# Twelve Strassen blocks in the first matrix, C11 begun by a copy between PSUM banks, and single score blocks in a re-ordered attention and MLP kernel

## The chip, the cores and the metric

The kernel runs on one NeuronCore of a Trainium2 chip. The metric is device time in microseconds, the median over runs; lower is better. A profiled execution gives a span, from the first to the last instruction, and the rows that this document quotes. Engines: PE is TensorE, DVE is VectorE, ACT is ScalarE, POOL is GpSimd, and SP is the SyncE queue that only issues DMAs.

## The reference

Windowed attention over 4 batches and 8 heads (768 positions, head size 64), then a two-matrix block with the gate h - tanh(h):

```python
scores = scale * np.matmul(q, k.transpose(0, 1, 3, 2))
keep = is_global | is_local        # 8 global keys, and the last 96 positions
scores = np.where(keep, scores + bias, -1e9)
a = softmax(scores)
attn = np.matmul(a, v)             # (4, 8, 768, 64) -> x: (3072, 512)
h = x @ w_in                       # 512 -> 2048
g = h - np.tanh(h)
out = g @ w_out                    # 2048 -> 512, float32
```

## The kernel before

**Turns.** The 3072 tokens are 24 tiles of 128, here called turns. Turns 0 to 3 are the first tiles of the four batches. A turn looks at its own keys and, unless it is the first of its batch, at those of the tile before, so it has one or two score blocks: 44 in all. Global keys are copied over the first 8 keys of the turns that no longer reach them (words K and V).

**Order.** Nothing is scheduled at run time. The string ORDER lists some thousand words, and every word issues one operation on its engine, in that order; HOMES gives each buffer and PSUM bank. Each engine runs its own instructions strictly in that order, so one that waits holds up all behind it on the same engine. A suffix names the engine where a word leaves a choice: `/a` ACT, `/d` DVE, `/p` POOL, `/s` SP.

**Attention words, for turn u.** `lq lk lv` load; the two first turns load float32 rows into a staging tile (keys from SP, queries from ACT; `load_rows`, L337) and `cq ck` cast them. `T`, `Te` transpose and copy out (turns 7 and up use a DMA transpose on SP). `B` adds the bias by matmul for the first four turns. `S` makes the scores: eight matmuls per block, with 64 rows in, in pairs on the two halves of the array (`a_S`, L391). `E` is the exponential on ACT, `M` the mask product on DVE, `AV` the product with v, `R` and `N` the normalisation, `X` and `Xe` the transposition of x (turns 8 and up by DMA on SP).

**First matrix.** Turns go in groups: 0 and 1 alone, 2 to 11 in pairs (groups 2 to 6), 12 to 23 in fours (groups 7, 8, 9). A plain unit is `m1` (matmuls, L477), `th` (tanh on ACT, L576), `g` (the gate on DVE, L590). For a group of four turns, a block of four feature tiles against 512 tokens may instead be a Strassen (Winograd) block: products `d1` to `d7`, each four matmuls of 256 columns (`in_product`, L522); copies `e0` to `e2` of a running sum in bank r (`d_copy`); adds `q11 q21 q22` (`d_add`, L544); sums of weights `v1` to `v4` for a block column and of tokens `y1` to `y4` for a group. DUNITS lists six such blocks: parts 1, 2, 3 of groups 8 and 9.

**Second matrix.** Always Strassen, over pairs of turns (2 x 2 blocks of 128 tokens, 1024 features, 256 outputs). `w1` to `w4` sum weights, `n1` to `n4` sum gates (`g_sum`, L619; n3 and n4 in place), `p1` to `p7` are products of eight matmuls each (`product`, L632), `a0 a1 a2` copy the running sum in bank r (`keep`, L650), `c11 c12 c21 c22` make the results (`result`, L653), `st` stores. Before, C11 is bank q (product 2) plus the copy a0 of product 1.

**Score runs.** From turn 8 on `S` takes three blocks at a time (THREES, L172 to L182); turns 4 to 7 take both of theirs at once. That makes 19 runs of score matmuls on PE.

Of the kernel before, what the change touches and what calls it, by code (L numbers as in the profile page):

```python
# [7 lines left out]
FP32 = mybir.dt.float32  # L8
# [9 lines left out]
lq.1 lk.1 zero rel ones.0 zero:7 dist lq.2 lq.0 lk.0 zero:7 zero:7 table lq.3 turn zero:7 first zero:7 lk.3 ident slopes  # L18
zero:7 zero:7 lk.2 ones.1 B.0 lv.1 cq.1/a ck.1/d bm.1 lv.0 T.1.1 em.1 lv.2 T.1.0 Te.1.1/d B.1 cq.0/a lv.3 Te.1.0/d
ck.0/a T.0.0 S.1 in.0 Te.0.0/a T.3.0 B.2 E.1.0 in.1 Te.3.0/d T.0.1 Te.0.1/d in.3 T.2.1 T.3.1 Te.2.1/a T.2.0 Te.3.1/d S.0  # L20
lq.4 Te.2.0/a AV.1 E.0.0 S.2 R.1 N.1/d in.2 B.3 E.2.0 lk.4 AV.0 S.3 R.0 N.0/d X.1 in.4 E.3.0 AV.2 Xe.1/d X.0 in.5 R.2
N.2/d bm.2 Xe.0/a AV.3 m1.1.0 lk.5 em.2 R.3 N.3/d X.2 m1.0.0 th.1.0 Xe.2/d X.3 lq.5 th.0.0 g.1.0 m1.0.2 Xe.3/a g.0.0
m1.1.2 th.0.2 m1.2.2 th.1.2 g.0.2 g.1.2 lv.4 m1.2.6 th.2.2 lk.6 g.2.2 T.4.0 th.2.6 m1.2.0 Te.4.0/a m1.1.4 lq.6 th.2.0
m1.0.4 lv.5 th.1.4 g.1.4 T.4.1 m1.2.4 Te.4.1/a g.2.0 th.0.4 S.4 th.2.4 g.0.4 out.1 m1.1.8 K.4/a E.4.0 g.2.6 m1.2.8
th.1.8 M.4.0 E.4.1 m1.0.8 g.1.8 th.2.8 out.0 M.4.1 m1.0.12 th.0.8 g.2.4 out.2 T.5.1 g.2.8 T.5.0 Te.5.1/a m1.1.12 out.3
Te.5.0/d th.0.12 g.0.8 S.5 lk.7 th.1.12 g.0.12 AV.4 E.5.0 g.1.12 lq.7 m1.2.12 n1.0/d E.5.1 lk.10 m1.2.10 M.5.0 lq.10
V.4/a R.4 m1.2.14 M.5.1 th.2.10 K.5/d N.4/d AV.5 th.2.14 T.6.1 X.4 R.5 Te.6.1/a T.6.0 N.5/d lq.9 Xe.4/a Te.6.0/d X.5 S.6
Xe.5/d g.2.14 m1.3.2 E.6.1 n3.0/d m1.3.10 g.2.10 lq.8 th.2.12 w1.1 th.3.2 p1.0 E.6.0 w1.0 m1.3.12 g.2.12 a0.0/a g.3.2
m1.3.4 lk.8 th.3.12 n2.0/d K.6/a th.3.10 m1.3.0 w2.0 m1.3.8 w4.0 w2.1 lk.9 p2.0 M.6.0 p6.0 lv.7 g.3.12 w3.1 T.7 m1.3.6
lv.6 a1.0/a c11.0 th.3.0 w3.0 p5.0 g.3.10 p7.0 a2.0/a n1.2/d th.3.4 g.3.0 p1.2 th.3.6 n2.2/d p2.2 a0.2/a w4.1 th.3.8  # L30
# [91 lines left out]
def kernel(  # L122
# [371 lines left out]
    def wsum(j, k):  # L494
        return four(("ws", j))[:, k - 1]
# [347 lines left out]
```

## Time and profile before

| What | Value |
|---|---|
| median of 3 runs | 203.38 us (201.31 to 203.54) |
| span of the profiled execution | 199.8 us |
| what the shown runs have beyond that span | 1.5 to 3.7 us |
| TensorE clock granted | 1.000 |
| busy PE, weight load, DVE, ACT, POOL | 193.1, 157.8, 178.6, 135.1, 75.3 us |
| DMA | 27.36 MB moved |

The profiled execution's own time is its span and what lies around it; the profile has no other figure for it.

How to read the rows. In the chain of waits a row is start, length, and what held the end of the program up at that time; `x16` counts instructions. In a table of waits: the waiting engine and line, what it waited for, the sum in us, how often, and the longest. In groups: line, engine, operation, output<-input, shapes and count, then busy time and the mean ns of one, then idle time before them. In windows each engine has its busy time and number of instructions. A DMA's landing is counted from its issue.

### The profile page before, as it was taken

The page shows a single profiled execution, that of the slowest core. Times are in us where ns is not written, and L with a number is a line of the kernel's source. Part 1 is how long each engine was busy: PE and PEld are TensorE (multiplying, and loading weights), DVE is VectorE, ACT ScalarE, POOL GpSimd, SP SyncE. Part 2 cuts the span into 40 slices and gives each one's busy share as a digit, 9 for nine tenths or more (in the row PEclk, how much of TensorE's full clock was granted, in tenths as well). Part 3 has the DMA queues.
Part 4 walks back from the last instruction along what each step waited for, and adds up shares of the span by engine and source line. Part 5 has one row for each costly group of instructions (what it writes and reads, how often), then busy time and mean ns, then how long its engine had stood idle before and what let it go on. Part 6 is the DMA issues. An engine that isn't in the chain of part 4 may idle for free.

```text
span 199.8 us, 5524 instructions
## 1 busy us (share of the span) xinstructions
PE 193.1 (97%) x2219; PEld 157.8 (79%) x2219; DVE 178.6 (89%) x348; ACT 135.1 (68%) x234; POOL 75.3 (38%) x97
## 2 busy tenths in 40 slices
PE   8799999999999999999999999999999999999992
PEld 2469998888888988988898655688898687888892
DVE  6487599999999999999999898999999999999942
ACT  3698898726569559758947789578778777464220
POOL 8987576350694057069207904702000100001110
PEclk9999999999999999999999999999999999999999
DMA  5999999999999999989996998994733101001233
GB/s 148 211 180 185 198 163 207 201 156 141 193 167 196 178 153 135 133 188 171 137 158 146 140 173 192 154 155 85 55 108 121 66 0 54 3 0 52 107 132 131
DMA packets 103545, 27.36 MB, mean 137 GB/s; under 512 B 93920, under 2 KB 101472, under 8 KB 103520
## 3 DMA queue, kind: packets, MB, share of 16 engines
q0 software_dynamic: 74048, 16.78, 89.5%
q1 hardware_dynamic: 28928, 9.70, 27.6%
q10 hardware_dynamic: 544, 0.52, 1.0%
q8 instruction: 17, 0.28, 0.5%
q14 instruction: 8, 0.07, 0.1%
HBM read 27.26 MB, written 6.29 MB: 168 GB/s over the span
## 4 chain that ended last, share of the span: by engine, by line
PE 85%; DVE 7%; DMA 3%; ACT 2%; issue 1%; ACTq 0%; DVEq 0%
PE ps L645 36%; PE ps L477 27%; PE ps L536 9%; PE ps L396 5%; PE ps L427 5%; DMA f<-in_q_dram 3%; DVE gall L590 2%; DVE x L444 2%; DVE mem L407 1%; PE ps L455 1%; ACT mem L403 1%; PE ps L320 1%; ACT mem L274 1%; PE ps L365 1%; ACT th L576 1%
## 5 line engine op out<-in xcount | busy, mean ns | idle before, releaser
L477 PE MATMUL ps<-xT,w_in_bf 128*128 128x256 bf16 (+2 forms) x544 | 69.0, 279 | 0.0
L477 PEld LDWEIGHTS <-w_in_bf 128*128 128x128 bf16 x544 | 47.2, 98 | 12.4
L576 ACT ACTIVATE th<-ps 128x512 f32<-128x512 f32 (+1 forms) x74 | 41.8, 591 | 18.7 <-PE ps L477 13.6
L590 DVE TENSOR_TENSOR gall<-ps,th 128x512 bf16<-128x512 f32 (+1 forms) x74 | 47.4, 668 | 6.0 <-ACT th L576 5.6
L645 PEld LDWEIGHTS <-gall 128*128 128x128 bf16 x488 | 46.4, 98 | 7.0
L662 POOL DMA_DIRECT2D out_dram<-ot x14 | 8.1, 580 | 102.5 <-ACT ot L274 52.4
L403 ACT ACTIVATE mem<-ps 128x1024 bf16<-128x1024 f32 x44 | 43.3, 1024 | 4.3 <-PE ps L396 4.2
L645 PE MATMUL ps<-w_out_bf,gall 128*128 128x256 bf16 (+1 forms) x296 | 36.3, 270 | 0.0
L274 ACT COPY sn<-ps 128x256 f32<-128x256 f32 x32 | 12.0, 375 | 20.3 <-PE ps L645 16.3
L645 PE MATMUL ps<-f,ss 128*128 128x256 bf16 x192 | 24.9, 273 | 0.0
L645 PE MATMUL ps<-wc,gall 128*128 128x256 bf16 x192 | 24.9, 273 | 0.0
L342 POOL DMA_DIRECT2D vb<-in_v_dram x24 | 21.5, 900 | 2.2 <-issue 1.0
L645 PEld LDWEIGHTS <-ss 128*128 128x128 bf16 x192 | 18.3, 98 | 2.8
L342 POOL DMA_DIRECT2D mem<-in_k_dram x20 | 17.9, 899 | 4.8 <-DMA w_out_bf<-in_moe_w_out_dram 3.1
L342 POOL DMA_DIRECT2D mem<-in_q_dram x20 | 18.1, 904 | 3.8 <-DMA w_out_bf<-in_moe_w_out_dram 3.0
L412 DVE TENSOR_TENSOR mem<-mem,mk 128x2048 bf16<-128x2048 bf16 x16 | 19.2, 1215 | 0.0
L659 DVE TENSOR_TENSOR ot<-ps,sn 128x256 f32<-128x256 f32 x36 | 14.7, 415 | 3.6 <-ACT sn L274 2.5
L444 DVE TENSOR_TENSOR x<-ps,rden 128x512 bf16<-128x512 f32 x23 | 15.8, 687 | 0.5
L274 ACT COPY mem<-ps 128x512 f32<-128x512 f32 (+1 forms) x22 | 12.7, 585 | 5.1 <-PE ps L536 3.9
L427 PEld LDWEIGHTS <-mem 128*128 128x128 bf16 x352 | 13.4, 97 | 2.1 <-ACT mem L403 0.5
L427 PE MATMUL ps<-vb,mem 128*128 128x65 bf16 x352 | 14.7, 193 | 0.0
L396 PE MATMUL ps<-mem 64*128 64x128 bf16 x352 | 13.1, 217 | 0.0
(78 smaller groups left out, 220.7 us busy)
## 6 DMA issues: line engine op xcount, KB each, us to landing
out_dram<-ot POOLq DMA_DIRECT2D x14, 256.0 KB, 2.8
vb<-in_v_dram POOLq DMA_DIRECT2D x24, 128.0 KB, 6.2
mem<-in_q_dram POOLq DMA_DIRECT2D x22, 128.0 KB, 6.3
mem<-in_k_dram POOLq DMA_DIRECT2D x22, 128.0 KB, 6.1
out_dram<-ot SPq DMA_DIRECT2D x9, 256.0 KB, 2.0
w_out_bf<-in_moe_w_out_dram POOLq DMA_DIRECT2D x4, 512.0 KB, 10.7
w_in_bf<-in_moe_w_in_dram POOLq DMA_DIRECT2D x4, 256.0 KB, 7.6
w_in_bf<-in_moe_w_in_dram POOLq DMA_DIRECT2D x2, 512.0 KB, 11.0
```

Source lines behind the costliest of these rows:

```text
L274: nc.scalar.copy(out=out, in_=in_)
L342: eng(e).dma_start(out=dst, in_=rows_of(src, u).rearrange("h p d -> p h d"))
L396: nc.tensor.matmul(bank(("s", u, o), hh)[:, p * P : (p + 1) * P], buf(("qk", back[u] if o else u))[r, 1, p, :], buf(("qk", u))[r, 0, p, :] ...
L403: nc.scalar.activation(d, banks(("s", u, o), 0, 1), AF.Exp, bias=0.0, scale=scale)
L412: nc.vector.tensor_tensor(out=t, in0=t, in1=mk[:, 1:3], op=ALU.mult)
L427: nc.tensor.matmul(t[:, h // (H // 2), h % (H // 2), :], buf(("p", u, o))[:, slot(h), :], buf(("v", back[u] if o else u))[:, h, 0 : Dh + 1 ...
L444: nc.vector.tensor_tensor(out=buf(("x", u)).rearrange("q (a h) d -> q a h d", a=2), in0=t[:, :, :, 0:Dh], in1=rden.to_broadcast([P, 2, H / ...
L477: nc.tensor.matmul(t[:, (f - f0) * n : (f - f0 + 1) * n], w_in_bf[j][:, c, fo : fo + P], x[:, c, 0:n], start=(c == 0), stop=(c == CD - 1),)
L536: nc.tensor.matmul(t[:, r * 2 * P : (r + 1) * 2 * P], w(r)[:, c], x[:, c], start=first and r + c == 0, stop=c == 1, skip_group_check=not f ...
L576: nc.scalar.activation(h_view(buf(("th", g, f0)), g, m), h_view(bank(("h", g, f0)), g, m), AF.Tanh, bias=0.0, scale=1.0)
L590: nc.vector.tensor_tensor(out=o, in0=v(h), in1=v(th), op=ALU.subtract)
L645: nc.tensor.matmul(bank((holder, a))[:, c0:c1], s(f), t(f)[:, c0:c1], start=first and f == 0, stop=f == HF - 1, skip_group_check=not first,)
```

## The change

The planner's ORDER and HOMES are new throughout, so nearly every engine's instructions stand in another order. The parts of the code:

- DUNITS has twelve blocks, all four parts of groups 7, 8 and 9. Plain `m1` units go from 74 to 50; each new block has seven products, three copies and two adds. Weight sums for part 0 and token sums for group 7 are added; the weight sums get a tile of their own, `ws`.
- C11 and q11 are no longer added by DVE. `a0` and `e0` copy bank r into bank q on ACT, and product 2 accumulates onto that (`first` is False). `q11` is gone; `c11` is a plain copy from bank q.
- The signs of the second matrix's sums are turned round so that n1 to n4 are all additions. Six `n3` and five `n4` become POOL DMAs that add onto their destination.
- A score block is a word of its own.
- `gall` keeps each turn's gates together, so a Strassen block's output is seen as two turns of 128 columns; `g_sum` then works on 1024 elements in a row.
- Fewer buffers: `mem` 20 for 23, `xT` 3 for 4, `ss` 3 for 5, masks 2 for 3. Stores go 4 to POOL and 22 to SP (before, 14 and 12).

```diff
-lq.1 lk.1 zero rel ones.0 zero:7 dist lq.2 lq.0 lk.0 zero:7 zero:7 table lq.3 turn zero:7 first zero:7 lk.3 ident slopes
+lq.1 lk.1 ones.1 rel lq.2 zero zero:7 zero:7 zero:7 zero:7 zero:7 zero:7 zero:7 turn slopes lk.0 lq.3 ones.0 dist lk.3
+first lk.2 ident cq.1/a bm.1 lv.1 lq.0 ck.1/d B.0 lv.0 em.1 T.1.1 lv.2 T.1.0 T.2.0 lv.3 Te.1.0/d Te.1.1/a B.1 Te.2.0/a
...
-    NM, NV, NG, NSS, NSN = 23, 12, 5, 5, 4
+    NM, NV, NG, NSS, NSN, NXT = 20, 12, 5, 3, 4, 3
...
-    DUNITS = [(8, 1), (8, 2), (8, 3), (9, 1), (9, 2), (9, 3)]
+    DUNITS = [(g, j) for g in range(7, 10) for j in range(4)]
...
-    gall = pool.tile([P, NG, CF, 2 * P], BF16, name="gall")
+    gall = pool.tile([P, NG, 2, CF, P], BF16, name="gall")
...
-    def a_S(xs):
-        for u, o in xs:
+    def a_S(u, o):
...
     def d_keep(g, j, k):
-        return buf(("k0", g, j)) if k == 0 else mems(("k12", g, j), FP32)[:, (k - 1) * 4 * P : k * 4 * P]
+        return d_bank(g, j, "q") if k == 0 else mems(("k12", g, j), FP32)[:, (k - 1) * 4 * P : k * 4 * P]
...
-            2: ("q", lambda r: w_in_of(a + r, 2), x_block(g, 2, 1), True),
+            2: ("q", lambda r: w_in_of(a + r, 2), x_block(g, 2, 1), False),
...
-        t = d_bank(g, j, part)
+        t = d_bank(g, j, part).rearrange("q (t r n) -> q t r n", t=2, r=2)
...
-                    t[:, r * 2 * P : (r + 1) * 2 * P], w(r)[:, c], x[:, c], start=first and r + c == 0, stop=c == 1,
+                    t[:, :, r, :], w(r)[:, c], x[:, c], start=first and r + c == 0, stop=c == 1,
...
     def d_add(g, j, k):
-        if k == 0:
-            q = d_bank(g, j, "q")
-            nc.vector.tensor_tensor(out=q, in0=q, in1=d_keep(g, j, 0), op=ALU.add)
-            return
...
-        eng(e).tensor_tensor(out=o(), in0=x(), in1=y(), op=op)
+        if e is POOL:
+            nc.gpsimd.dma_start(out=o, in_=y, accum_op=ALU.add)
+        else:
+            eng(e).tensor_tensor(out=o, in0=x, in1=y, op=ALU.add)
...
-            2: ("q", lambda f: g_of(a, HF + f), w(1, 0), True),
+            2: ("q", lambda f: g_of(a, HF + f), w(1, 0), False),
...
     def keep(e, a, k):
-        copy(e, buf(("sn", a, k)), bank(("r", a))[:, 0:DH2])
+        copy(e, buf(("sn", a, k)) if k else bank(("q", a))[:, 0:DH2], bank(("r", a))[:, 0:DH2])
...
-        if (i, j) == (1, 2):
-            copy(e, o, bank(("r", a))[:, c0:c1])
+        if i == 1:
+            copy(e, o, bank(("qr"[j - 1], a))[:, c0:c1])
             return
-        holder, k = {(1, 1): ("q", 0), (2, 1): ("z", 1), (2, 2): ("z", 2)}[i, j]
-        nc.vector.tensor_tensor(out=o, in0=bank((holder, a))[:, 0:DH2], in1=buf(("sn", a, k)), op=ALU.add)
+        nc.vector.tensor_tensor(out=o, in0=bank(("z", a))[:, 0:DH2], in1=buf(("sn", a, j)), op=ALU.subtract)
```

Three places in the instruction order. First, ACT at the start of the program, where the query rows of turns 1 and 0 are loaded into the staging tile (`f32`) and cast into `mem`; `mk` is a mask and `ps` PSUM. Before:

```order
L339 DMA f32_80<-in_q_dram 128x2x256 x2
L274 ACT_TABLE_LOAD
L274 CAST mem_81<-f32_80 128x512
L325 ACTIVATE mk_68<-ps_61 128x1024
L274 CAST mem_81<-f32_80 128x512 x2
L274 CAST mem_81<-ps_61 128x512
```

In the change:

```order
L332 DMA f32_80<-in_q_dram 128x2x256
L267 ACT_TABLE_LOAD
L267 CAST mem_81<-f32_80 128x512
L332 DMA f32_80<-in_q_dram 128x2x256
L318 ACTIVATE mk_68<-ps_61 128x1024
L267 CAST mem_81<-ps_61 128x512 x2
L267 CAST mem_81<-f32_80 128x512
```

The second query load, turn 0's, has moved behind the cast of the first, which waits for the first load to land.

Second, PE in the middle of the program: a score run (L396 before, L388 now) between matmuls of the second matrix (L645) and of Strassen blocks of the first (L529 now). Repeats are left out. Before, three blocks, 24 matmuls, in one run:

```order
L645 LDWEIGHTS ss_103
L645 MATMUL ps<-f_80,ss_103 128x256
L396 LDWEIGHTS mem
L396 MATMUL ps<-mem 128x128
...
L645 LDWEIGHTS ss_104
L645 MATMUL ps<-f_80,ss_104 128x256
```

In the change, one block, eight matmuls, between two products of a Strassen block:

```order
L529 LDWEIGHTS w_in_bf_74
L529 MATMUL ps<-xT_99,w_in_bf_74 128x2x128
L388 LDWEIGHTS mem
L388 MATMUL ps<-mem 128x128
...
L529 LDWEIGHTS ws
L529 MATMUL ps<-mem,ws 128x2x128
```

The runs have become shorter and there are 27 of them where there were 19; the output of a block matmul is now two runs of 128.

Third, POOL late in the program: loads of v (`vb`), stores (`ot`), and in the change the sums n3 and n4 (into `gall`). Before:

```order
L342 DMA mem_81<-in_k_dram 128x8x64
L342 DMA vb2_84<-in_v_dram 128x8x64
L342 DMA vb5_87<-in_v_dram 128x8x64
L662 DMA out_0_dram<-ot0_113 128x512
L342 DMA vb4_86<-in_v_dram 128x8x64
L342 DMA vb6_88<-in_v_dram 128x8x64
L662 DMA out_0_dram<-ot3_116 128x512
L342 DMA vb7_89<-in_v_dram 128x8x64
```

In the change:

```order
L624 DMA gall_102<-ss0_103 128x1024
L335 DMA vb0_82<-in_v_dram 128x8x64
L335 DMA vb1_83<-in_v_dram 128x8x64
L657 DMA out_0_dram<-ot0_111 128x512
L624 DMA gall_102<-ss2_105 128x1024
L335 DMA vb3_85<-in_v_dram 128x8x64
L624 DMA gall_102<-ss1_104 128x1024
L624 DMA gall_102<-gall_102 128x1024
```

Sums of gates stand between the last loads of v, and behind a store.

More of the change, by code (lines that the diff above doesn't have):

```diff
@@ L734 @@
             op(("Xe", u), SP, lambda e, u=u: a_DX(u))
-    for n, xs in enumerate(runs):
-        op(("S", n), PE, lambda e, xs=xs: a_S(xs))
+    for u in range(NU):
+        for o in blocks_of(u):
+            op(("S", u, o), PE, lambda e, u=u, o=o: a_S(u, o))
     for g, us in enumerate(groups):
@@ L758 @@
         for k in range(3):
-            op((f"e{k}", g, j), None, lambda e, g=g, j=j, k=k: d_copy(e, g, j, k))
-        for w, k in (("q11", 0), ("q21", 1), ("q22", 2)):
+            op((f"e{k}", g, j), None if k else ACT, lambda e, g=g, j=j, k=k: d_copy(e, g, j, k))
+        for w, k in (("q21", 1), ("q22", 2)):
             op((w, g, j), DVE, lambda e, g=g, j=j, k=k: d_add(g, j, k))
```

281 lines of the change are left out of this document (139 added, 142 removed).

## The prediction

> **What bounds the kernel now.** I read the page first: busy shares, the 40 slices and the chain that ended last.
>
> ```profile
> PE 193.1 (97%) x2219; PEld 157.8 (79%) x2219; DVE 178.6 (89%) x348; ACT 135.1 (68%) x234; POOL 75.3 (38%) x97
> PE 85%; DVE 7%; DMA 3%; ACT 2%; issue 1%; ACTq 0%; DVEq 0%
> ```
>
> TensorE holds 85% of the chain. A busy TensorE may still be waiting inside its rows, so the chain in order of time and TensorE's own waits come next.
>
> ```profile
> 1.48 6.26 DMA f<-in_q_dram
> 7.76 0.63 ACT mem L274
> ...
> 8.44 0.40 PE ps L361 x4
> ...
> 41.83 1.75 PE ps L645 x16
> ...
> 52.31 0.55 PE ps L396 x16
> ...
> 62.61 0.78 PE ps L396 x24
> 63.39 1.85 PE ps L645 x16
> ...
> 114.20 4.32 PE ps L477 x20
> ...
> 143.74 3.06 PE ps L536 x28
> ...
> 178.65 17.12 PE ps L645 x160
> 195.80 0.42 DVE ot L659
> ```
>
> ```profile
> PE ps L361 <- ACT mem L274: 1.2, 1, 1.2
> PE ps L455 <- DVE x L444: 0.9, 3, 0.4
> ```
>
> The chain starts with the second query load, waits 1.2 us for its cast at 8.44, and then TensorE loses only 0.9 us, in three places, until its last product ends at 195.80. So a microsecond of matmul time is a microsecond of the kernel, unless another engine takes over. The windows name the candidate.
>
> ```profile
> core 0: us, PE busy (x) PEld busy (x) DVE busy (x) ACT busy (x) POOL busy (x), PEclk, DMA share, GB/s
> 115.00:135.00 20.00, 20.00 (x200) 12.61 (x198) 19.29 (x38) 15.59 (x33) 5.86 (x8) 1.00 1.52 168
> 135.00:155.00 20.00, 20.00 (x233) 16.95 (x231) 19.99 (x35) 16.29 (x28) 1.46 (x2) 1.00 0.47 94
> 155.00:175.00 20.00, 20.00 (x166) 16.01 (x164) 19.98 (x32) 13.74 (x24) 0.58 (x1) 1.00 0.07 29
> ```
>
> VectorE is as full as TensorE from 115 to 175 us, so work given to it is not free. ScalarE has a quarter of its time left; GpSimd has nearly all.
>
> **Term 1, six more Strassen blocks on TensorE: -2.4 us.** A plain block of the first matrix is 16 matmuls of 512 columns. The chain has 20 of them in 4.32 us, 0.216 each, so 3.46 us. A Strassen block is 28 matmuls of 256 columns; the chain has just 28 in 3.06 us. Each block saves 0.40, six save 2.4. The new output order (two runs of 128 columns instead of one of 256) I take as free; see the rivals.
>
> **Term 2, single score blocks: +1.5 us.** Sixteen score matmuls take 0.55 us and 24 take 0.78, so eight cost 0.23 and a run 0.09 besides (0.55 less twice 0.23). A product of 16 behind a score run takes 1.85 us where it takes 1.75 elsewhere: 0.10 more. A run therefore costs 0.19 beyond its matmuls. The score matmuls stay 352. Their runs on TensorE, counted in the order, go from 19 to 27: 8 x 0.19 = 1.5. That takes back most of term 1.
>
> **Term 3, the start: +0.4 us.** ScalarE now issues the second query load only behind its first cast, and VectorE casts what lands.
>
> ```profile
> 4.06 0.62 ACT L274 CAST mem<-f 128x512 bf16<-128x512 f32 x1 [0.63 <-DMA f<-in_q_dram]
> L276 DVE CAST mem<-f x1: 785/785/785, 4.7 to 4.7; 128x512 bf16<-128x512 f32 x1
> L339 ACTq DMA_DIRECT2D f<-in_q_dram x2: 640/674/707, 0.7 to 1.5; - x2
> DMA to landing us min/median/max: 3.3/5.1/6.4
> 8.77 0.40 PE L396 MATMUL ps<-mem 64*128 64x128 bf16 x8
> 9.09 0.41 PE L365 MATMUL ps<-turn,mem 128*64 128x128 bf16 x8
> 9.44 0.60 PE L320 MATMUL ps<-slopes,dist 128*128 128x512 bf16 x2
> 9.88 0.39 PE L361 MATMUL ps<-turn,mem 128*128 128x128 bf16 x4
> ```
>
> The issue moves from 1.45 to 4.06 + 0.62 = 4.68 us. These four loads land 3.3 to 6.4 us after issue. Alone on its queue but beside GpSimd's loads, this one is between; I take 4.4, so it lands at 9.1, is cast by 9.9, and the transposes of turn 0 start there instead of at 8.44: 1.5 later. Before them TensorE now does one transpose half of turn 2, the first score block and one bias pair; by the starts of the four matmul rows that is 0.35 + 0.32 + 0.44 = 1.1 us brought forward. The net is +0.4. With 3.3 it is -0.7, with 6.4 it is +2.4.
>
> **Term 4, C11 begun in PSUM: 0 on the path.** The first product's bank is copied to the bank in which the second accumulates, so product 2 now waits for a copy; VectorE loses the add. No row has a copy from bank to bank; the bounds are these.
>
> ```profile
> L274 ACT COPY sn<-ps 128x256 f32<-128x256 f32 x32 | 12.0, 375 | 20.3 <-PE ps L645 16.3 <-DVE ot L659 3.4 <-DVE mem L509 0.5
> L274 ACT COPY mem<-ps 128x512 f32<-128x512 f32 x18 | 10.3, 585 | 4.1 <-PE ps L536 3.9
> L547 DVE TENSOR_TENSOR ps<-ps,mem 128x512 f32<-128x512 f32 x6 | 4.1, 687 | 0.0
> L550 DVE TENSOR_TENSOR mem<-ps,mem 128x512 f32<-128x512 f32 x12 | 8.2, 682 | 0.0
> L659 DVE TENSOR_TENSOR ot<-ps,sn 128x256 f32<-128x256 f32 x36 | 14.7, 415 | 3.6 <-ACT sn L274 2.5 <-PE ps L645 0.8
> ```
>
> VectorE's add into PSUM and into SBUF cost alike (687, 682 ns), so I take ScalarE's SBUF prices, 375 and 585 ns; below, nothing is gained, since ScalarE is not the bound; above, 0.69. The cover is what TensorE does between the two products: in the order never under eight matmuls of 256 columns, 0.87 us (products 1 and 2 of pairs 12 and 16; blocks d1 and d2 of group 9, part 0). A copy that starts at once fits. If ScalarE is 0.5 us late in each of the 24 places it does not, and some tenths are lost each time, with the whole in-order TensorE queue behind.
>
> **Term 5, the other engines: 0.** VectorE's prices:
>
> ```profile
> L630 DVE TENSOR_TENSOR ss<-gall 128x1024 bf16<-128x1024 bf16 x12 | 8.2, 684 | 0.1
> L590 DVE TENSOR_TENSOR gall<-ps,th 128x512 bf16<-128x512 f32 x70 | 45.8, 682 | 5.5 <-ACT th L576 5.2
> L568 DVE TENSOR_TENSOR gall<-ps,th 128x1024 bf16<-128x1024 f32 x6 | 7.3, 1219 | 0.0
> L509 DVE TENSOR_TENSOR mem<-w_in_bf 128x512 bf16<-128x512 bf16 x5 | 2.1, 413 | 0.0
> L444 DVE TENSOR_TENSOR x<-ps,rden 128x512 bf16<-128x512 f32 x23 | 15.8, 687 | 0.5
> ```
>
> It loses 11 sums of the second matrix (0.68: 7.5 us), 9 C11 adds (0.415: 3.7), 6 q11 adds (4.1), 2 normalisations (1.4), and 24 gates of 512 become 12 of 1024 (1.8): 18.5. It gains 12 q21 and q22 adds (8.2), 4 weight and 4 token sums (3.3) and 5 block copies (3.4): 14.9. Net -3.6 of 178.6, so it does not become the bound over the whole; in the order it stays level with TensorE around groups 7 and 8, so no slack opens either. ScalarE gains about 13 block copies (7.6) and 9 C11 copies (3.4), and stays under 150 of 200. Ten stores move from GpSimd's queue to SP's, where transposes of later turns stand behind them; a store that waits for its results delays these, which TensorE needs several microseconds later.
>
> The three waits of 0.9 stand before transposes of x, which VectorE's normalisation feeds. In the order, turns 5 and 7 now have about 0.4 us more matmul work between their attention product and that transpose, so their waits go; turn 4 has two groups of eight matmuls less there (1.7 us) and may get one. I put the new small waits at the same sum.
>
> **Sum.** -2.4 + 1.5 + 0.4 = -0.5: a span of 199.3 for 199.8. The shown runs have a median of 203.38, 3.5 above that span (the lowest, 201.31, only 1.5), so I forecast **202.9**.
>
> **Rivals.** *Late accumulating DMAs (slower).* Eleven sums become a GpSimd DMA that adds onto its destination. A product reads the result, and every later matmul stands behind it. Nearest rows:
>
> ```profile
> DMA to landing us min/median/max: 1.7/2.3/5.8
> out_dram<-ot POOLq DMA_DIRECT2D x14, 256.0 KB, 2.8
> w_in_bf<-in_moe_w_in_dram POOLq DMA_DIRECT2D x2, 512.0 KB, 11.0
> ```
>
> Same size, same queue, same row length: 2.8 us, with 1.7 and 11.0 as ends. In the order, pairs 10 and 12 have 4.9 us of matmul work between product 2, which frees the block, and product 3, which reads it; pairs 14 and 18 have 5.7, pair 20's other sum 5.2. So it decides from 4.9 us on. At 7 us the waits are 2.1 + 2.1 + 1.3 + 1.3 + 1.8 = 8.6, and the time 211.5; it passes 2% from about 6.2 us. Against it: 2.8, and DMA engines nearly idle there (0.07 to 0.47 of 16). The Trainium skill's page "DMA: Bandwidth & Descriptors", section "Anatomy of one DMA", gives about 2 us fixed plus bytes over 436 GB/s, by which I estimate 2.6 us for 256 KB; by that figure nothing waits, and no run here shows an accumulating DMA.
>
> *Thin covers (slower, within 2%).* VectorE as full as TensorE, a new copy ahead of product 2, SP's stores ahead of transposes: if half of the 24 copies lose 0.2 us, and the start takes its upper bound, that is 2.4 + 2.0 over the forecast: up to 207. For it speaks VectorE at 19.98 of 20.
>
> *More gained (faster, within 2%).* The query load lands in 3.3 us (-1.1 against my term) and the 0.9 us of waits go: 200.9.
>
> *Strided output.* Writing two runs of 128 slows the 336 block matmuls. If each doubled (0.109 to 0.216), that is +36 us, 239. No row has such an output. Against it, score matmuls write runs of 128 columns at 0.03 us each. By the Trainium skill's "PSUM — Partial Sum Buffer", section "Specifications (TRN2)", any pattern that is not contiguous slows matmuls significantly; no run shows it yet.
>
> *Nothing changes*: VectorE's order sets the pace and the matmuls saved become waits: 203.4 to 205, inside the range.
>
> **How the numbers follow.** Forecast 0.50, thin covers 0.18, more gained 0.16, nothing 0.06, late accumulation 0.08, strided output 0.02. The range 200.4 to 205.9 leaves out the two slow cases, the end of the thin covers, and a little below the fast case. About 2%, 4 us, is what a measurement tells from no change. Faster than 199.3 needs more than all gains together, 0.06; slower than 207.4 is late accumulation, strided output and a bit of thin covers, 0.11; the rest, 0.83, lies within.
>
> **What would show it.** Right: 28 block matmuls in 3.06 us, score runs of 8 near 0.23 with 0.1 on either side, the first transposes of turn 0 between 9 and 11 us, TensorE's waits under 2 us in all, accumulating DMAs landing in under 4.9 us. Wrong: TensorE waiting for a DMA before product 3 or 7, or for ScalarE's copy before product 2, block matmuls above 0.11 us, or VectorE rows as the end of the chain in the middle of the kernel.

## The result, and the profile after

The change is slower: 210.47 us in the median of 6 runs (208.20 to 211.62), where the kernel before has 201.64 (201.24 to 203.54) beside it; the ratio is 1.040, 95% interval 1.034 to 1.045. The ratio leaves out the slowest run of the change, which was in a slower state, and it is not the quotient of the two medians. The forecast was 202.9, in a range of 200.4 to 205.9. The profiled execution of the change took 208.2 us, with a span of 206.4 at a granted clock of 1.0; its other executions have spans of 207.8 to 209.8 at clocks of 0.984 to 0.992, so the profile shows the shortest of them.

The page after: busy time, TensorE's and the DMA engines' rows of 40 slices, and the chain's shares.

```profile
PE 193.9 (94%) x2291; PEld 163.9 (79%) x2291; DVE 176.9 (86%) x336; ACT 145.1 (70%) x257; POOL 79.2 (38%) x98
PE   7679999999999987899999999989999999999992
DMA  6999999999999999999999999592537613903644
PE 35%; issue 6%; DMA 2%; DVE 2%; ACT 1%; POOLq 0%
```

TensorE's row has gaps in the third slice (10 to 15 us) and in slices 15 to 17 (72 to 88 us); before, it was 9 in all but the first two and the last. The DMA engines are at 90% or more from the second slice to the 25th, which ends at 129 us. They were nearly as full before, a row that the prediction did not read:

```profile
DMA  5999999999999999989996998994733101001233
```

The longest of TensorE's waits in the change, without the warm-up's (waiting engine and line, what it waited for, us in all, times, longest):

```profile
PE ps L354 <- DVE mem L269: 2.3, 1, 2.3
PE ps L469 <- DMA xT<-x: 1.1, 1, 1.1
PE ps L641 <- DVE ot L654: 0.7, 1, 0.7
PE ps L388 <- DMA mem<-mem: 0.7, 1, 0.7
PE ps L641 <- DMA gall<-ss: 0.6, 1, 0.6
PE ps L388 <- ACT sn L267: 0.4, 1, 0.4
```

Before there were two such rows beside the warm-up's, 1.2 and 0.9. No row names ScalarE's copy from bank to bank. The last row is put down to a ScalarE copy, but it stands before turn 7's scores at 54.95, and turn 7's transpose had landed at 54.91. So of the 3.5 us that these rows have after the start, 2.8 end at the landing of a DMA, and the 0.7 behind VectorE ends at one too, as shown below. The chain of waits, late in the program:

```profile
133.39 5.08 DMA gall<-ss
138.47 0.05 issue
138.52 1.05 PE ps L641 x8
...
141.31 0.33 PE ps L388 x8
...
154.99 3.49 PE ps L529 x32
...
187.04 15.75 PE ps L641 x152
```

Block matmuls still take 0.109 us each (3.49 / 32), a single score block 0.33, the last product ends at 202.79 (195.80 before).

**Where the time went.** Each word of the order is laid beside its matmuls' start in both traces, and its time compared with the shortest that its shape has elsewhere; what it has beyond that is called lost. The first packed unit of the first matrix (group 1, feature tiles 2 and 3) starts at 16.75 us before and at 18.92 in the change: +2.2 at the start. From there on the matmuls themselves are about 0.7 us shorter (terms 1 and 2 together: -0.9), and TensorE loses about 6.8 us where it was 1.7: +5.1. Together 2.2 - 0.7 + 5.1 = 6.6, the difference of the spans. The 2.2 and the 4.4 that follow are read from the traces; how the 4.4 divides moves by about half a microsecond with what is counted as the same shape. The rows above name 3.5 of the 6.8.

The start, in time (start, length, engine, and in brackets the idle time before):

```profile
4.75 0.61 ACTq L332 DMA_DIRECT2D f<-in_q_dram  x1
...
10.59 0.43 DVE L269 CAST mem<-f 128x512 bf16<-128x512 f32 x1 [2.88 <-DMA f<-in_q_dram]
...
11.07 0.62 PE L354 MATMUL ps<-turn,mem 128*128 128x128 bf16 x8 [2.35 <-DVE mem L269]
```

The second query load is issued at 4.75, as worked out, and its cast starts at 10.59: 5.8 us, not 4.4.

The middle. Busy time from 70 us on, before and then the change:

```profile
core 0: us, PE busy (x) PEld busy (x) DVE busy (x) ACT busy (x) POOL busy (x), PEclk, DMA share, GB/s
70.00:80.00 10.00, 10.00 (x148) 8.62 (x147) 9.49 (x21) 7.38 (x13) 6.71 (x8) 1.00 1.56 143
```

```profile
70.00:80.00 10.00, 8.56 (x124) 7.21 (x117) 7.78 (x16) 8.54 (x17) 3.14 (x4) 1.00 1.55 216
80.00:90.00 10.00, 8.90 (x132) 7.45 (x130) 9.42 (x20) 6.81 (x13) 6.53 (x8) 1.00 2.20 150
```

TensorE and VectorE both stand idle from 70 to 80 us, so neither is full there. The DMA share sums the packets' times, so above 1 it says that on average more than one packet per engine is under way. VectorE's own list of waits has this row in the change and none like it before:

```profile
DVE ot L654 <- DMA out_dram<-ot: 2.0, 1, 2.0
```

C22 of pair 2 goes into the staging buffer that the store of turn 2 reads, and that store stands behind transposes on SyncE's queue. TensorE's wait of 0.7 for VectorE (`ot`, above) is for this C22.

Why transposes matter now is seen by laying their issues (SPq) beside the score runs that read them. Before: the transposes of turns 12, 13, then 15 and 14.

```profile
63.82 1.92 SPq L377 DMA_TRANSPOSE mem<-mem  x1
...
68.56 1.23 SPq L377 DMA_TRANSPOSE mem<-mem  x1
...
78.59 5.20 SPq L377 DMA_TRANSPOSE mem<-mem  x2
```

From turn 8 on the number of an `S` word in the kernel before counts runs of three blocks and not turns: S.10 is the first to read turn 12, S.11 turn 13, S.12 turns 14 and 15. These three runs:

```profile
73.13 0.84 PE L396 MATMUL ps<-mem 64*128 64x128 bf16 x24
...
77.99 0.84 PE L396 MATMUL ps<-mem 64*128 64x128 bf16 x24
...
89.47 0.84 PE L396 MATMUL ps<-mem 64*128 64x128 bf16 x24
```

The change: transposes of turns 12 and 13, then 15, then 14; the scores of turns 13, 12, 15, then 14 with 12.

```profile
65.99 4.54 SPq L370 DMA_TRANSPOSE mem<-mem  x2
...
71.27 2.05 SPq L370 DMA_TRANSPOSE mem<-mem  x1
...
74.05 2.14 SPq L370 DMA_TRANSPOSE mem<-mem  x1
```

```profile
74.79 0.40 PE L388 MATMUL ps<-mem 64*128 64x128 bf16 x8
...
76.10 0.40 PE L388 MATMUL ps<-mem 64*128 64x128 bf16 x8
77.21 0.40 PE L388 MATMUL ps<-mem 64*128 64x128 bf16 x8 [0.72 <-DMA mem<-mem]
...
80.18 0.62 PE L388 MATMUL ps<-mem 64*128 64x128 bf16 x16
```

Median landings of transposes at 62 to 88 us before:

```profile
mem<-mem SPq DMA_TRANSPOSE x6, 5.5
xT<-x SPq DMA_TRANSPOSE x4, 3.4
```

In the change, at 64 to 80 us:

```profile
mem<-mem SPq DMA_TRANSPOSE x4, 6.1
xT<-x SPq DMA_TRANSPOSE x2, 4.4
```

The four transposes are issued within 8 us in the change, 66 to 74, where they took 17 before, 64 to 81, and the first scores that read them follow sooner: from issue to first scores there were 9.3, 9.4, 8.3 and 10.9 us for turns 12 to 15, and there are 10.1, 6.8, 6.1 and 5.9. The landings themselves changed less: 5.6, 4.8, 5.4 and 7.2 us before, 7.6, 6.3, 5.5 and 5.9 now. So the time to spare between landing and first scores was 3.7, 4.6, 2.9 and 3.7 us; it is now 2.5, 0.5, 0.7 and 0. It is 0 too for turn 7's transpose and for turn 8's transposed x in the change. Slack was not large before either: turn 7 had 0.7 us, and the x of group 5 had 1.5.

### The profile page after: what moved, and what is told of

The parts are those of the page before. It is cut to its first block, busy times and chain, and to the rows that moved or that the text cites. A ratio compares the mean times of both kernels' runs of the same rounds, so it can differ in the third digit from the quotient of the medians.

```text
span 206.4 us, 5687 instructions
## 1 busy us (share of the span) xinstructions
PE 193.9 (94%) x2291; PEld 163.9 (79%) x2291; DVE 176.9 (86%) x336; ACT 145.1 (70%) x257; POOL 79.2 (38%) x98
## 2 busy tenths in 40 slices
DMA packets 105770, 30.26 MB, mean 147 GB/s; under 512 B 94096, under 2 KB 101648, under 8 KB 105744
## 5 line engine op out<-in xcount | busy, mean ns | idle before, releaser
L469 PE MATMUL ps<-xT,w_in_bf 128*128 128x256 bf16 (+1 forms) x448 | 46.9, 257 | 1.4 <-DMA xT<-x 1.1
L469 PEld LDWEIGHTS <-w_in_bf 128*128 128x128 bf16 x448 | 37.6, 98 | 6.2 <-DMA xT<-x 1.4
L581 DVE TENSOR_TENSOR gall<-ps,th 128x512 bf16<-128x512 f32 (+1 forms) x50 | 31.6, 662 | 3.9 <-ACT th L566 3.8
L566 ACT ACTIVATE th<-ps 128x512 f32<-128x512 f32 (+1 forms) x50 | 27.3, 584 | 9.0 <-PE ps L469 6.5
L335 POOL DMA_DIRECT2D mem<-in_q_dram x20 | 18.3, 916 | 21.5 <-DMA mem<-mem 12.9
L529 PEld LDWEIGHTS <-ws 128*128 128x128 bf16 x192 | 18.5, 98 | 2.9 <-DVE mem L507 0.3
L529 PE MATMUL ps<-mem,ws 128*128 128x256 bf16 x144 | 20.1, 273 | 0.1
L624 POOL DMA_DIRECT2D gall<-ss x5 | 4.3, 865 | 38.3 <-PE ps L641 38.3
L539 DVE TENSOR_TENSOR mem<-ps,mem 128x512 f32<-128x512 f32 x24 | 16.1, 684 | 0.7 <-PE ps L529 0.5
L267 ACT COPY ps<-ps 128x256 f32<-128x256 f32 (+1 forms) x24 | 11.2, 472 | 7.7 <-PE ps L529 4.4
L388 PE MATMUL ps<-mem 64*128 64x128 bf16 x352 | 14.7, 218 | 1.3 <-DMA mem<-mem 0.7
L267 ACT COPY sn<-ps 128x256 f32<-128x256 f32 x20 | 7.6, 378 | 11.5 <-PE ps L641 11.2
## 6 DMA issues: line engine op xcount, KB each, us to landing
w_out_bf<-in_moe_w_out_dram POOLq DMA_DIRECT2D x4, 512.0 KB, 10.9
```

The costliest lines, as they stand in the source:

```text
L267: nc.scalar.copy(out=out, in_=in_)
L335: eng(e).dma_start(out=dst, in_=rows_of(src, u).rearrange("h p d -> p h d"))
L388: nc.tensor.matmul(bank(("s", u, o), hh)[:, p * P : (p + 1) * P], buf(("qk", back[u] if o else u))[r, 1, p, :], buf(("qk", u))[r, 0, p, :] ...
L469: nc.tensor.matmul(t[:, (f - f0) * n : (f - f0 + 1) * n], w_in_bf[j][:, c, fo : fo + P], x[:, c, 0:n], start=f == f0 and c == 0, stop=(c = ...
L529: nc.tensor.matmul(t[:, :, r, :], w(r)[:, c], x[:, c], start=first and r + c == 0, stop=c == 1, skip_group_check=not first or r > 0,)
L539: nc.vector.tensor_tensor(out=a, in0=d_bank(g, j, "z"), in1=a, op=ALU.add)
```

## The experiments

Times are medians, ratios are to the kernel before on the same chip. "Lost" is TensorE's time beyond the shortest, after the start, as above (about 6.8 in the change, 1.7 before).

**The start.** `early_load` puts the query load back and gives it a staging row of its own:

```diff
-... rel lq.2 zero ... bm.1 lv.1 lq.0 ck.1/d       f32.0.q:0
+... rel lq.2 lq.0 zero ... bm.1 lv.1 ck.1/d       f32.0.q:3
```

> The change, with turn 0's query load issued directly behind turn 1's, into a staging row of its own. Theory A (the places add up: 2.2 us lost before the first gate matmuls, the rest later): the transposes of turn 0 start near 8.6 us instead of 11.1, the span is 2 to 2.4 us shorter than 206.4, and the granted clock is 1.00 in all runs, so that the runs lie near 206. Theory B (the accumulating DMAs make the loss): the start moves but later waits take it back, span 205.5 to 206.4. Theory C (the order is tight everywhere, a repaired place gives back less than half): span 205.3 or more.

Measured: 207.99 us, 1.032 (1.028 to 1.036); span 205.5, all runs at clocks of 0.996 to 1.0. The first packed unit starts at 17.17. So the late load costs about 2 us (1.6 by the ratios, 2.5 by the medians); the rest, most of the loss, stays. The profiled span fell by only 0.9, less than the 2 to 2.4 expected, though the start came 1.7 us earlier, since more was lost later. Its lost time is 7.6: 0.7 and 1.2 around the scores of turns 12 and 15, 1.2 before the first unit of turns 8 and 9, 1.6 before block product d6 of group 7, and smaller ones.

`before_late_load` does the opposite to the kernel before:

```diff
-lq.1 lk.1 ... lq.2 lq.0 lk.0 ...      f32.0.q:2
+lq.1 lk.1 ... lq.2 lk.0 ... cq.1/a lq.0 ...   f32.0.q:0
```

> The kernel before, with turn 0's query load moved behind the first cast and into the same staging row, as the change has it; nothing else. Theory A: the transposes of turn 0 start 2 to 2.7 us later than 8.44, and the span grows by as much, to about 202; if the idle time of TensorE there also lowers the granted clock, the clock falls below 1.00 and the time rises by 3 to 5 us. Theory B or C: the order before has slack behind the start, under 1 us.

Measured: 206.88 us, 1.027 (1.023 to 1.030). There the load alone costs 5 us: TensorE has nothing to do meanwhile, and the granted clock is lower. The clock in its 40 slices:

```profile
PEclk9969999999999999999999999999999999999999
```

The transposes of turn 0 in its time line:

```profile
11.05 0.61 PE L361 MATMUL ps<-turn,mem 128*128 128x128 bf16 x4 [4.42 <-ACT mem L274]
```

TensorE waits 4.42 us for 1.2 before, and in the third slice the granted clock is 0.6. In the profiled execution, span 203.6 at a clock of 0.992, all of the 3.8 us over the page of before stand ahead of the first packed unit (20.54 for 16.74), 3.2 of them in this wait. Its other executions have clocks of 0.980 to 0.982 and spans 1.0 to 1.5 us longer; the kernel before has 0.996 to 1.0.

**Accumulating DMAs.** `sums_dve` puts all eleven sums back on VectorE (`n3.x/p`, `n4.x/p` become `/d`).

> The change, with the eleven sums that GpSimd adds by DMA done by VectorE, at the same places in the order. Theory A (they cost only the one wait of 0.7 us, and VectorE has no room): between 0.5 us faster and 2 us slower than the change. Theory B: 4 us or more faster, near the kernel before.

Measured: 218.23 us, 1.080 (1.074 to 1.086), with 14.3 us lost. Without the DMAs the change is 8 us slower still, so VectorE has no room for these sums. That does not price the DMAs themselves; TensorE's only wait for one in the change is the 0.6 above.

**SyncE's queue.** `stores_pool` gives the stores of turns 4, 2 and 0 to GpSimd (`/s` to `/p`).

> The change, with the three stores of turns 4, 2 and 0 issued by GpSimd instead of the SP queue, where they stand between DMA transposes. Theory A (the SP queue is the bound from 66 to 79 us, each store takes 0.65 us of it): the waits of 0.9 us before the score block of turn 15 and of 1.3 us before the first matmuls of group 5 shrink by 1.5 us together, span near 204.9. Theory B: no change, within 0.3 us. Theory C: under 0.7 us.

Measured: 209.82 us, 1.041 (1.036 to 1.046): no change that can be told. The wait for turn 8's x went, those before turn 15's scores (0.9 to 1.3) and for the token sums of group 7 (0.2 to 1.5) grew.

`early_stores` is `early_load` with the stores where SyncE is idle; `after_stores` the same on the change itself:

```diff
-c12.2/a S.9.1 ... st.2.0/s ... st.0.0/s ... st.3.0/s ... st.5.0/s
+c12.2/a st.0.0/s st.2.0/s S.9.1 ... c21.4 st.3.0/s st.5.0/s ...
```

> The change with the early query load, and with four stores moved in SyncE's order alone: those of turns 0 and 2 directly behind the copy that completes turn 2 (their data are ready before the transposes of turns 12 to 15 are issued), those of turns 3 and 5 behind the transpose of turn 8's x, where SyncE is idle for 7 us. Nothing else differs from the run with the early load (205.5 us of span). Theory 'SyncE's queue': the store of turn 2 stood behind a row of transposes; VectorE's result C22 of pair 2 writes the same staging buffer and waited 2.3 us for that store to land, and TensorE's product 4 behind it 1.2 us; the stores also put off the transposes that TensorE and the token sums wait for. Then VectorE's 2.3 us wait goes, the 1.2 us before product 4 goes, the waits for the transposes of x (1.2 and 1.6 us) shrink by half or more, and the span falls to 202.5 to 203.5. Rival 'VectorE is the bound': the waits come back as waits for VectorE and the span stays within 0.7 of 205.5.

> The change with the same four stores moved in SyncE's order, and the query load left late. If start and queue are separate causes the gain is the same as with the early load: 2 to 3 us against the change (208.2 in the profiled run, 210.5 median). If the late start hides it, or VectorE is the bound, under 0.7.

Measured: 209.21 us, 1.036 (1.030 to 1.042), and 213.00, 1.056 (1.052 to 1.059). The first cannot be told from `early_load`, the second is slower than the change. VectorE's wait for the store is gone, but the four transposes that followed now land after 7.3 us (median) and TensorE loses 1.6 us before turn 8's attention product and 2.4 before turn 15's scores. So these orders of the queue do not mend it.

**VectorE.** `early_nomask` leaves out eight turns' mask products:

```diff
-op(("M", u), DVE, lambda e, u=u: a_MM(u))
+op(("M", u), DVE, lambda e, u=u: a_MM(u) if u < 8 or u > 15 else None)
```

> The change with the early query load, and without the mask products of turns 8 to 15 on VectorE (six to eight operations of 1.22 us, about 9 us of VectorE between 60 and 100 us); those turns' masked scores are left in. Rival 'VectorE is the bound in the middle': the waits in the middle (about 5.5 us) go nearly all, the span falls by 3 us or more from 205.5. Theory 'SyncE's queue': VectorE itself waits there (2.3 us for a store, 2.4 us for a transpose), its relief is lost in those waits, and the span falls by under 1 us.

Measured: 207.21 us, 1.028 (1.024 to 1.032), not told from `early_load`; span 206.3.

```profile
60.00:70.00 10.00, 10.00 (x135) 8.54 (x130) 6.14 (x13) 9.52 (x16) 4.38 (x5) 1.00 2.17 153
70.00:80.00 10.00, 8.57 (x133) 6.88 (x129) 6.74 (x16) 7.46 (x16) 5.39 (x7) 1.00 1.35 212
80.00:90.00 10.00, 8.89 (x121) 7.89 (x122) 6.20 (x15) 7.11 (x13) 4.23 (x5) 1.00 2.26 157
```

VectorE falls to two thirds (third number of a row) and TensorE stands as idle as before. VectorE is not the bound there.

**Is it the transposes?** `early_const` lets the scores of turns 12 to 15, the units of turns 8 and 9 and the blocks of group 7 read constant tiles; every DMA stays.

```diff
+slopes[r, p, :] if 12 <= u < 16 else ...      # both operands of a_S
+x = w_out_bf[0] if g == 5 else buf(("xT", g)) # m1; x_block for g == 7
```

> The change with the early query load, where the scores of turns 12 to 15 read a constant tile in place of the transposed queries and keys, and the plain units of turns 8 and 9 and the Strassen blocks of group 7 read a weight tile in place of the transposed x (so these parts are not computed from their data); every DMA is still issued. TensorE and the token sums then wait for none of these DMA transposes. Theory 'the transposes of turns 12 to 15 and of x 8, 9, 12 to 15 come too late': the waits at those places go, 0.7 + 1.2 + 1.6 and part of the 1.2 behind a store; span 201.5 to 203. If the cause is elsewhere: above 204.8.

Measured: 206.12 us, 1.022 (1.019 to 1.026), span 204.4. The span lies between the two theories. The waits at these places went, 3.5 us, but 1.9 us came of it (by the medians): the one behind the store of turn 2 grew from 1.2 to 1.8, and others came, such as 1.0 before turn 19's scores.

**Is it the loads?** `early_noloads` leaves out GpSimd's loads of q and k of turns 16 and 18 to 22 and of v of six turns.

> The change with the early query load, without GpSimd's loads of the queries and keys of turns 16 and 18 to 22 and of v of turns 12, 14, 16, 17, 19 and 20 (those turns are computed from older rows in the same buffers). In the run with the early load, transposes issued while such loads run land 5 to 6 us after issue, against 2.3 to 3.6 alone. Theory 'loads hold up the transposes': turn 8's x and turn 15's x land in 2.5 to 3.6 us, the waits of 1.2 and 1.6 us behind them go, span 202.3 to 203.5; the waits of the scores of turns 12 and 15 stay. If the loads do not matter: within 0.7 of 205.5.

Measured: 209.97 us, 1.041 (1.037 to 1.046). Not what I expected: the loads that were left no longer waited for buffers and came at 71 to 76 us, in front of the transposes of x. Landings at 75 to 79 us, and at 88 to 104, when GpSimd loads nothing:

```profile
q0 software_dynamic: 2693, 0.34, 132.7%
...
xT<-x SPq DMA_TRANSPOSE x2, 7.9
```

```profile
q1 hardware_dynamic: 6176, 1.97, 63.6%
...
xT<-x SPq DMA_TRANSPOSE x6, 2.4
mem<-mem SPq DMA_TRANSPOSE x3, 3.3
```

7.9 us beside loads, 2.4 without, for the same kind of transpose. And TensorE loses nothing from 88 to 139 us, where `early_load` loses 2.4. At 80 to 90 us it stands 3.3 us at one place, and the clock falls to 0.83 of that window.

`early_slots` loads turns 12 to 15 earlier, into four more slots:

```diff
-NM ... = 20     kq.12:12 kq.13:11 kq.14:5 kq.15:6
+NM ... = 24     kq.12:20 kq.13:21 kq.14:22 kq.15:23
-lk.11 ... lv.9 ... lk.13 lq.12 lk.12 lq.13 ... T.12 T.13 st.4.0/s T.15 st.2.0/s T.14
+lk.11 lq.12 lk.12 ... lv.9 lq.13 lk.13 lq.15 lk.15 ... T.12 T.13 st.2.0/s T.15 T.14 st.4.0/s
```

> The change with the early query load, and with four more slots in the tile of queries and keys, made room for by one weight-sum tile in place of four (block products 3, 5, 6, 7 read plain weights, the sums are still made, so the first matrix of groups 7 to 9 is not the reference's). Turns 12 to 15 are loaded into the new slots as soon as GpSimd comes to them, ahead of the loads that waited for a free slot, and their transposes stand together in SyncE's order ahead of the stores of turns 2 and 4. Theory 'the buffers that the change gave up put off the loads': turn 12's transpose is issued 4 to 6 us earlier than 63.7, the waits before the scores of turns 12 and 15 and behind the store go, about 2 us, span 203 to 204. Rival 'the transfers themselves are full there': the earlier loads lengthen the transposes of turns 8 to 11, new waits appear before 65 us, span 205 or more.

Measured: 213.68 us, 1.059 (1.053 to 1.065), the rival's case. But the run does not test earlier transposes as it should: turn 12's transpose is issued at 69.2 us, later than the 63.7 of `early_load`, as its output goes where turn 11's rows lie until they are transposed. So it still waits for turn 11's, which now lands after 9.7 us (8.6 in `early_load`); those of turns 9 and 10 take 8.6 and 10.9 (5.2 and 7.6), and turn 7's attention product waits 2.9 us for its v. Its start also came 2 us later (19.12 for 17.17). The waits before the scores of turns 12 to 15 are gone; these have 1.2 to 5.9 us to spare.

**The order.** `early_order` moves some ten words by hand (p4.2 and p4.4 ahead of S.12.1 and S.15.0, g.4.4 and g.4.6 ahead of c22.2, st.2.0 ahead of T.13, p2.6 ahead of m1.5.0, d2.7.0 and m1.6.0 ahead of d6.7.0); in places a word now writes a PSUM bank that another still uses, so part of its output is not the reference's.

> The change with the early query load and with a few words of the order moved by hand, so that other work stands where TensorE waits: products 4 of pairs 2 and 4 ahead of the score blocks of turns 12 and 15, two gates ahead of the two C22 results on VectorE, the store of turn 2 ahead of turn 13's transpose on SyncE, product 2 of pair 6 ahead of the plain unit that waits for turn 8's x, and block product d2 and a plain unit ahead of d6 of group 7, which waits for the token sums. Theory 'no slack': the transposes land when they land, and only the order lacks something to do meanwhile; of the 4.7 us lost at those four places in the run with the early load (0.7, 1.2, 1.2, 1.6) 2 to 3.5 us go, span 202 to 203.5. Rival 'the transfers set the pace': later transposes come later too, the waits return behind, span above 204.8.

Measured: 209.67 us, 1.039 (1.036 to 1.042). The waits moved: 1.9 us before p4.2, 1.3 behind turn 14's scores, 1.2 before d6. Some of that is the hand-made order's own, so it tells only that a few words do not mend it.

**Size of the loads' pieces.** `early_rows` and `before_rows` load q and k in pieces of four rows:

```diff
-load_natural(e, buf(("kq", u))[:, j, :].rearrange("q (h d) -> q h d", h=H), src, u)
+load_rows(e, buf(("kq", u))[:, j, :].rearrange("q (b f) -> q b f", b=2), src, u)
```

> The change with the early query load, where GpSimd's loads of queries and keys of turns 4 to 23 take four rows of 64 in one piece, as those of the first turns do, in place of one row: the same bytes, a quarter of the pieces. The rows then lie in other places of the tile and nothing sets them right, so the scores of these turns are not the reference's; every other instruction stands where it stood. Theory 'the DMA engines are full': the profile's DMA row is 9 to about 110 us, transposes that are issued while loads run land 5 to 9 us after issue; with a quarter of the pieces they land in 2.3 to 4 us, the 4.7 us of waits for transposes and for the store go nearly all, and the span falls from 205.5 to between 200 and 202. Rival 'the transposes among themselves, SyncE's queue': they still land in 5 us or more and the span stays above 204.

> The kernel before with the same edit to the loads of turns 4 to 23 (scores of these turns not the reference's). There the transposes of turns 12 to 15 land 20 us and more ahead of their scores, so both theories expect a span within 1 us of the kernel before: 198.5 to 200.

Measured: 206.08 us, 1.020 (1.015 to 1.026), and 202.21, 1.001 (0.996 to 1.006). The same bytes in 75,050 packets instead of 105,770 give the change 1.9 us by the medians (1.020 for 1.032) and the kernel before nothing. The expectation for the kernel before rests on 20 us to spare, which is wrong; it had 2.9 to 4.6 us there, and that was enough. The trace does not show where the 1.9 us came from: the profiled execution is the slowest of the four, span 204.9 for 205.5, and 0.5 of these 0.6 us are at the start. The waits at the scores of turns 12 and 15 fell to 0.3 us there, but those before turn 8's unit and before d6 grew, from 1.2 and 1.6 to 1.7 and 2.5, and the time lost is as before, 7.7. Less came than expected: turn 12's transpose lands in 5.9 us for 7.4, but turn 15's x in 7.0, as it is issued while loads of v, in small pieces still, begin. The Trainium skill's page "DMA: Bandwidth & Descriptors", section "Specifications", wants 512 B or more per transfer for full rate; the direction agrees, and no run here shows that threshold.

**Holding the loads back.** `early_gate` lets GpSimd wait for turn 8's and turn 15's transposed x before the two bursts of loads; `early_gate_rows` adds it to `early_rows`.

```diff
-Xe.8 lk.16 ...           lq.20 Xe.15 ...
+Xe.8 gate.8 lk.16 ...    Xe.15 gate.15 lq.20 ...
+nc.gpsimd.dma_start(out=gate[0:1], in_=x_dst(u)[0:1, 0])
```

> The change with the early query load, and with two gates in GpSimd's order: a copy of 256 bytes that waits until turn 8's transposed x has landed stands ahead of the burst of loads that began at 75.2 us, and one that waits for turn 15's transposed x ahead of the burst that began at 97.4 us. All is computed as in the change. Theory 'GpSimd's loads hold up the transposes': the transposes of x issued just ahead of these bursts land in 2.3 to 4 us in place of 5.3 and 6.3, the waits of 1.2 and 1.6 us behind them shrink to under 0.5 each; the delayed loads may cost something later (their scores had 2 to 4 us to spare). Span 202.8 to 204.5 against 205.5. If loads do not matter the two landings stay above 5 us and the span does not fall.

> The same two gates together with the loads of queries and keys in pieces of four rows (scores of turns 4 to 23 not the reference's). If loads and transposes getting in each other's way is the whole of the waits between 65 and 112 us, the sum of the two gains is seen: span 200.5 to 202.5, with TensorE's lost time after 17 us under 4 us in place of 7.6. If the waits only move on to later transposes: 203.5 or more.

Measured: 212.69 us, 1.051 (1.041 to 1.060), and 207.25, 1.024 (1.014 to 1.033). Landings of the transposes of x at 75 to 79 us in `early_load`:

```profile
xT<-x SPq DMA_TRANSPOSE x2, 4.9
```

In `early_gate`:

```profile
xT<-x SPq DMA_TRANSPOSE x2, 3.4
```

Its longest waits of TensorE:

```profile
PE ps L389 <- DMA mem<-mem: 4.0, 3, 2.1
PE ps L420 <- DMA vb<-in_v_dram: 3.5, 2, 3.1
```

The half of the theory on landings holds: turn 8's x in 2.9 us for 5.3, turn 15's in 2.6 for 6.3, and the waits behind them are gone. The other half, that the loads can wait, does not: behind the gates TensorE waits 1.7 us for turn 19's transpose, at 121.46, and 3.5 for v, of which 3.1 at 92.39. The other 2.1 of the first row stand before turn 15's scores at 75.87, ahead of the first gate, which is issued at 79.53; there turn 15's transpose landed after 6.9 us where it took 5.6 in `early_load`, with the same instructions ahead of it. So this landing differed by 1.3 us between two executions, and a wait of that size in one trace need not come from the edit. With the smaller pieces too (`early_gate_rows`, span 204.4) nothing is gained that can be told from `early_rows`: the case in which the waits only move on.

**C11 alone.** `before_c11` makes this one part of the change in the kernel before:

```diff
-copy(e, buf(("sn", a, k)), bank(("r", a))[:, 0:DH2])
+copy(e, buf(("sn", a, k)) if k else bank(("q", a))[:, 0:DH2], bank(("r", a))[:, 0:DH2])
-2: ("q", ..., True)      -p1.2 ... p2.2 a0.2/a
+2: ("q", ..., False)     +p1.2 p7.0 ... a0.2/a p2.2   # and so in five other pairs
```

> The kernel before with one part of the change alone, in the second matrix: the copy of product 1 goes from bank r to bank q, product 2 accumulates on it, and C11 is a plain copy from bank q on VectorE in place of an add. Products 1 and 2 of some pairs are moved by one or two words, so that other matmuls lie between them. If the copy costs nothing on the path (term 4): within 0.7 us of the kernel before. If TensorE waits for the copy: 12 waits of 0.2 to 0.5 us, 2.4 to 6 us slower.

Measured: 206.50 us, 1.025 (1.020 to 1.030). Where bank q has another user between a0 and product 2, the C11 of that pair is not the reference's, and TensorE waits 0.7 and 0.6 us for such copies; the rest of the 4.9 us I did not settle. It says that this part cannot be had for nothing in an order not made for it, and nothing on the change, whose own list has no such wait.

No run points to a version that beats the kernel before; the best variants of the change stay 2% above it.

## Why the prediction was wrong, step by step

**Term 5 failed**: "a store that waits for its results delays these, which TensorE needs several microseconds later", and with it "I put the new small waits at the same sum". What TensorE loses is about 5.1 us more. That transposes are needed later held for the kernel before, where those of turns 12 to 15 had 2.9 to 4.6 us to spare; in the change they have 0 to 2.5. The prediction counted what moved on each queue, and not when TensorE comes to use it. In the order it could be seen: in the change the first scores of turns 12 to 15 all stand ahead of group 5's first unit; before, only turn 12's did, turn 13's stood behind that unit, and those of 14 and 15 behind the group's last.

What the runs show in its place: the DMA engines are busy for 90% or more of the time for some 120 us in the change, and not much less before; a transposed tile lands 2.4 to 3.3 us after issue when GpSimd loads nothing, and up to 9 beside loads (10.9 in `early_slots`); and the change's order leaves less time than that takes. With VectorE a third idle the middle waits as much (`early_nomask`), and neither of the two other orders of the stores mends it (`early_stores`, `after_stores`). The transposes' landings are part of it: when the scores, units and blocks no longer read them, 1.9 us come back (`early_const`). Loads beside them lengthen the landings (`early_noloads`, `early_gate`), and each time one transfer is helped, waits return elsewhere.

Not shown is the greater part of the sum: the late load and the landings give back some 2 us each, and of the 8.8 us between the medians about half has no run that gives it back (the best variant, `early_rows`, is still 4.4 behind). One candidate is a part of the change that the prediction put at nothing without a word, the fewer buffers. In the change GpSimd's twenty query loads wait 21.5 us in all, 12.9 of them for transposes that free their buffers; before, they wait 3.8. `early_slots`, with four more, also changed the order of the loads and does not settle what that costs.

**Term 3 was mis-sized.** The mechanism, a second load behind the first cast, was right; its cast began 5.8 us after the issue, not 4.4, and the step cost 2.2 us in the profiled execution, within its bounds (-0.7 to +2.4), not +0.4. `early_load` gives back 1.7 of the 2.2. Unforeseen was the clock: five of six executions of the change have 0.984 to 0.992 over the whole run and spans 1.4 to 3.4 us longer than the profiled one; with the early load they have 0.996 to 1.0. The clock does not explain these spans alone: 207.8 goes with 0.984, and 209.1 and 209.8 with 0.992. The shared staging row, which kept the load behind the cast, could have been read in HOMES.

**Terms 1 and 2 were right**: about -0.7 together for -0.9; block matmuls at 0.109 each and single score blocks at 0.33 with 0.10 around them.

**Term 4 was right in the change**: 12 and 12 copies at the prices that I took (375 and 585), and no wait for them on TensorE.

```profile
L267 ACT COPY ps<-ps 128x512 f32<-128x512 f32 x12 | 6.9, 577 | 4.4 <-PE ps L529 4.4
L267 ACT COPY ps<-ps 128x256 f32<-128x256 f32 x12 | 4.3, 367 | 3.2 <-PE ps L641 1.8 <-DVE gall L557 0.9 <-ACT ot L267 0.5
```

VectorE was relieved by 1.7 us, not 3.6, which decided nothing.

**The rivals.** Late accumulating DMAs: they land in 4.0 us,

```profile
gall<-gall POOLq DMA_DIRECT2D x6, 256.0 KB, 4.0
gall<-ss POOLq DMA_DIRECT2D x5, 256.0 KB, 4.0
```

above the 2.8 of the stores and below the 4.9 from which they decide; the longest, 5.08, cost 0.6 us. The estimate of 2.6 from the Trainium skill's page "DMA: Bandwidth & Descriptors", section "Anatomy of one DMA", was too low; the measurement decides. Strided output: no cost, 0.109 us per matmul, against the rule in the Trainium skill's "PSUM — Partial Sum Buffer", section "Specifications (TRN2)"; for two runs of 128 float32 the measurement decides. Thin covers came nearest: a slower kernel by waits and a start near its upper bound. It named the stores ahead of transposes too, but it priced only the copies, at 2.4 us; the waits came at the landings of DMAs, twice as large. Against late accumulation the prediction said that the DMA engines are "nearly idle there (0.07 to 0.47 of 16)"; the share is measured against all 16 engines together, so 0.47 is nearly half of them.

## What to carry to other kernels

When an order is searched anew, lay for each transfer its landing beside the first instruction that uses it, before and after: the time to spare that is lost there shows in no busy share. Count the runs that read a tile by what they read, and not by their number in the order. Read the DMA engines' row of the profile before calling a moved transfer hidden; in the runs here that helped one transfer while the row stood at 9, another came later. And look at the clock of all executions: in `before_late_load` 3.2 us more of waiting at the start went with 5.4 us more in the medians and with lower clocks.

## What the runs showed of the hardware

- An idle stretch of TensorE of 4.4 us at the start went with a granted clock of 0.6 in a slice of 5 us and with 0.98 to 0.99 over the run (`before_late_load`); one of 3.3 us in the middle went with 0.83 in a window of 10 us (`early_noloads`); in the change's profiled execution one of 2.35 us at the start went with 1.0.
- DMA transposes of the same size land in 2.4 us when GpSimd loads nothing and in 7.9 beside its loads (medians, `early_noloads`), and the issue of one on SyncE takes 1.2 us alone and up to 3.4 in a row (4.2 in `early_slots`).
- The landing of one transpose differed by 1.3 us between two runs with the same instructions ahead of it (5.6 in `early_load`, 6.9 in `early_gate`).
- Adding 256 KB from SBUF onto SBUF by a GpSimd DMA takes 4.0 us in the median of eleven, 1.2 more than a store of that size did before.
- A matmul that writes two runs of 128 float32 to PSUM takes as long as one that writes 256 in a row: 0.109 us in both.
